# Causal attention with a gated feed-forward on one core: scores in four column groups of 32 keys, odd heads in turned order, and a new recorded order

## The chip, the cores and the metric

The kernel runs on one core of a Trainium2 chip. The metric is the device time of one execution in microseconds. Of an execution the profiler also gives a trace: which instruction ran when on which engine, and what it waited for.

## What is computed

A linear recurrence with complex decay runs over 768 steps for 4 x 8 heads of 48 channels; its result, reordered to 3072 rows of 384, goes through two weight matrices with a rational function between them.

```python
B, H, S, D = 4, 8, 768, 48                     # q, k, v, a_re, a_im: (B, H, S, D)
mag = np.sqrt(a_re * a_re + a_im * a_im)
scale = np.minimum(mag, 0.999) / (mag + 1e-06)
a_re_n, a_im_n = (a_re * scale, a_im * scale)
for t in range(S):
    S_re, S_im = (ar * S_re - ai * S_im + k_t v_t^T, ar * S_im + ai * S_re)
    y[:, :, t] = np.einsum('bhd,bhde->bhe', q[:, :, t], S_re)
x = y.transpose(0, 2, 1, 3).reshape(B * S, H * D)
h = x @ w_in                                   # (3072, 384) @ (384, 2048)
P = a[0] + a[1] * h + a[2] * h**2 + a[3] * h**3
Q = 1.0 + np.abs(b[0]) * np.abs(h) + np.abs(b[1]) * h**2
out = (P / (Q + 1e-06)) @ w_out                # (3072, 2048) @ (2048, 384)
```

## The kernel before, in words

The 768 steps are cut into six chunks of 128, and each chunk with each of the four batches is a unit, 24 in all. Two units make a pair, and each pair has one feed-forward pass over its 256 rows.

A unit goes through four helpers. `norm` (L441) loads `AA`, normalizes the decay and runs its product along the chunk. `angle` (L471) sums the angles. `outer` (L509) loads `QK` and `V`, forms the rotated queries and keys and writes them by DMA into `HQ`, whose 96 used partitions are 2 x 48 channels. `attn` (L539) is the part that the change touches. For each of two groups of four heads it transposes the keys (`turn`, L552) into `kT`, then forms the scores of 128 keys by 128 queries (`scores`, L563), which VectorE multiplies by the mask `cmask` out of PSUM into `ST`. `values` (L581) multiplies the scores by `V` and, from the second chunk on, the queries by the state `St`; these matmuls write 32 output partitions each, in four column groups of the array. L585 forms the state's update out of `kT` and `V`, again 32 output partitions at a time. `ffn` holds the two feed-forward matmuls, L613 into `ph` and L630 into `po`, with the rational function on ScalarE and VectorE between them.

Every fp32 matmul call leaves two records in the trace (384 records at L563 for 24 x 2 x 4 calls).

All steps are operations of a plan: each has a list of the engines that could run it with an assumed cost, and reads and writes that order it. The order of all 2,731 operations, and the engine of each, is not worked out at run time but stands in the string `ORDER`, which `recorded` (in the listing) decodes: base85, inflated, 16-bit steps; of a sum the lower 12 bits are the operation's number, the rest the place of its engine in the operation's list. If the string fits the plan, its order is taken and the assumed costs play no part. Each engine executes its operations in that order.

PSUM tiles of `attn` come from a ring named `at` with two buffers of one bank each.

Of the kernel before, what the change touches and what calls it, by code (L numbers as in the profile page):

```python
# [42 lines left out]
VP = 64  # L43
STAGE = ("wh0", "g", "wh1", "g", "wh2", "g")
# [171 lines left out]
def act(n, psum=False):  # L216
# [11 lines left out]
    "GRstTugEM7K99&7@|oTOgW}>-r=8N3d+9Qee8y@g`I4$c%VOyz4?>e<89QH=GCb#Nj8~x18ZN50Bw8QHU9F_QOOzJ#d<_GwU!@rM7Bj!Q`#RDr<}d4*A<mQh"
    "P-XA7F4Hku0Q!~5x4d^h6w(~gnES4ngv(3R=vCdQe@bz=8yXy+o)yO3-sWQ$Cx5W}BbqP0bdwY{x7{$EODx5S`!ntpkq5e2!nBJ#F7xG<P9yuGQbm$<orb{w"
    "arw8rsB5Gfne37F>e(~?5zxvZ>j5!&Zj}t;{cd_2#B#Xmr`x16D|gTjwVW3&&zTKw1~o~S!AiBwO~0nZ*%5w>H-uG7gMA7ZgvsZunXF0D58SWo1FdLhx=6{4"  # L230
    "Nyy2LDe&K+@)f*(y2C4>oprhws|)p{deWGE;=I?ifsA11rE)4XSDHu<@8i%Z@ED?vWta@mW%8kBnl;XWnWN$*<P}{F0|#@pMCOulr1aqJ3z8Zd?d=Mkr(%`m"
    "n%0nux>nxNi(H-7W7<oO>k4mP=%W6m6=6yzaK9{Xhi+<ZJI)oC5xUZ5xhS1!-garcwMbsq>e9h`KlBmVS7o)2WE!<llkP^sws?EVU(Y`IGAR^kN9L>z&5%AC"
    "FI%LOro!|2`k6Mdy>imD9C5Uh#yZ1h>molB?rhNR5=jir<Ol60zv)pO2v3K)yHsVlj*+EWPZr1rtk6tqpoR?CenSJD{;DTUzMn$v7wCST7$LRDYd>)v)#f<C"
    "WprL%`$!2HEc0}WCR+9P=_r`DO<$7bCdwtttMU>1JR)D|E*YmM^gFm%1%7qLWxC01Tg88<gFw{jO8vra^N(s>)?2ERWV0@mw#3#}#-Z1hnkaj0HKHj69tGOP"
    "zT&sXNxI0>`m3Gk-@}`B5>*%ZQHSyT=UQ4eNIkfBR$A#T)7^z|yL;?<mkbWtd44K+?xs#%{MT7?x{j7>p`WCcS?)^7C|RS|WsNz6BZbLaxIaRQqPq7@n)KD<"
    "ZWXMGk3X38l}YhO%0itiPvS<saE=<%m27&+Dm1nOuSnIC(p=VSEmoXskNB%JMLyP{cD<jY@9KH(_LMs8)W@GJJ>_woA=AO>m^toulb7JZWPK7J>974*H&^@M"
    "vHMJC_lv$sRaZ-_oQ-)eXPBPVzs#@xAsvEe?1kwq;c`EDhREKK-{KZ#t-yyjYX|vRKektIua*O_t(u%PwcH=t6z99h|Ih1ql(<al*u8F{c86E*Yj0^uy^fmZ"
    "ZX<8sL)qaH1u7No0=Hd1*8Vbpr+zjw5bUFps_TiMJ5lY@TK0nPv=xlHsw1?wZRRSn!$Ex-79Z3B_~>DMU|P96lj~p9rzF57PfwWB{xEt{f;?fiy7xg+b%}1W"
    "YyDU_I9|TcS+=u3h(0z6j;y3wJ<V7buV?53Wo3)jrtfSbqMhRDmvo57WH^2`TX)%Yel-bd|BG7GP?z^cqr-M)Kc2H+4~TDG(7pKCl*0Or!?{!C6xkH$JoBtO"
    "sgFr>o9>6h;mvS&vz(*@Hn6#V7V3<a>e2`#$LUo$qDM?)_dJ!)*T(ig{y45Y880WO@U^(utdjJyhI$N?he&HyPSb{R43?i#-?Y?+t}Pjt#a(xruI`>zgFzjs"  # L240
    "dpK(QPS3{Na~)99U%1iN=3SSeRpVP^ZPs?I`2@=BVr#kG+Lf56;~(wGJBn}Kk&Q9QIXmg>PfA8ix13CL-c3fc?;71_m-vzN<TqszF?2-nrFq+v3EJI0@T*7y"
    "PBo8eF9GQhaAUoB-W|eEuIorR=Id7ZR+pRJE<kL84kz{@teXG_D$yDC=}x-YM|Pi|jVE3(!^!qvtaj97YFGT{cg-;4+!9mH^}{<m+a>OVt~E7XNg{d*^x8^0"
    "Ft1B}K96ga)yKB;2XNOz2Rl(^2ReCm@SFn5&0te;YFrmZKhJdo>Y1-I^@vvV(zFG>mB>m>K`D*Nqn12H|D49tmo!%XkI5z+eJ`ME?w~R=aO(~Fr0wGJG>xg|"
# [12 lines left out]
    "+HWpx%|7=I44P${y2ECL`xpIpHyr&IG^dg`{;uos^+{CxkX~St*r`|e+XTm$Plp-AeEfuK1a|o-vA(^-<lKU}X)VrD9+k!N+*LkNTst#R4*9`Zx-3d~h?^hw"
    "+rZBKoMewMy+ld_iI0CgYZ{K(QYzaUx4(r^Z?ak=`-vaS7vp8Pndx3<-fJqGO<2xUO=J$Agu@(Sdij4mpI{<Pz<-M}t=<8j<M8k@m^}~2%Tk%j?D8c%t7<<("
    "y>vM|=qaYVN_g0M`gp1~kxtaRHyP#WulV4<wGqyA1Ai<4>uU6fqxusXm_dd;aLj$w;XJ5!M7QUt?i|@*deDJ-GHVWEmpr&|oNpo|l_|YAihG8hGLmVsI6l{w"
    "sedY{9zpXvb%WjR|I^HNfwzy+E4G+hkJCP+m)@d=$<*qA&L+DbwFi~2;L4-e5%|m?-c82!s}f@u{4D5>cksCgfj_3aOOmxHZ3JB~P))4NM=#Ck=<CTb$!7YT"
    "?0CK_h$InPF1THTE3IXb)YYc;B(v>HVAL2*3}C8gYQtO=vW-F|o%o!`GY;UP4v&qHL-G$I%Frg9^S(2!-H)t?3*c@|G{e5)g30hS@0OIMrj$!5Jk4y<km=;^"  # L260
    "=plVwvWTP{+PK0*H59~dYVgaz8anI(bb1A}I-;s@dD%Yg*9VzgeVH2WLe*uNJnAu@{EZmv75++eg5KEyel#b_EKYK(m?TbczUqOpqCmJNy62?LZqYnlz<F`3"
    "1XIborlFfhB#$wP-7r1fHo8Ls_1K|TVaz}{8HqEe^XxY`eK84GzcFCA3wqF6aA?eovCQ80fB4_8OL@$RZ}N>-IOBV0D)7X+dK;ICkYCIg_XWzhLq#6)Ml4g~"
    "_TYCdW|;<fP8+h>#%bhH_Z1!!OJAwS`LsOiTti70xED?x{~+Fc-G&!c#$|WG-HLeT2~^yXC%2MEG$__)?<o4+V{m0VtSK#*jVE>7rNW33<s2TG&fFHsvq{{!"
    "ZnpV7SvPp6NugR+-~bU|Frjb~h=i4Wag+_A1ztIj?2i(aX{?SU;pjt%JUBfS=x=24K67mWHLO8Ao0*7ex!||EC^>KLpzs2C{sO-F6Dt0RXJY7g7wCyeC@l=O"
    "W)fK(YWC!JzOBpuOA}Lt!e3P?^Y%$jAC)EE-G*@r1|`U#At(k{9`(72v&M3L1>A$*4Qg_Aw-B2G4H$3}HIzhM<!l*PdX@?W(Va&BL6%W`A5_4T@5v+|j%K67"
    "r&;NHs+e0?iGVx#rmWj$UUFY+WlqX%sAmk0l&^uJg7tEVvKH%CU?Mt;dlnE=F4$+|=7I9^K_ikA?ZZN5+)_t`hD!ehKKc0Cr3Y1tL`raa%7@X#QC*Z2hYcP)"
    "d|-;X;NuZxaojCL9g0%B2O3nslm7yi-+c@"
# [4 lines left out]
def attn_moe(ctx: ExitStack, tc: tile.TileContext, qk, aa, v, w_in, w_out, coef, heads, lanes, out):  # L272
# [10 lines left out]
    cmask = cst.tile([P, P], F32, name="cmask")  # L283
    make_identity(nc, cmask)
    nc.scalar.activation(ident, cmask, AF.Copy)
    nc.gpsimd.memset(cmask, 0.25)
    nc.gpsimd.affine_select(out=cmask, in_=cmask, pattern=[[1, P]], compare_op=ALU.is_ge,
                            fill=0.0, base=0, channel_multiplier=-1)
    smask = cst.tile([P, 2 * NJ, C], BF16, name="smask")
    nc.vector.memset(smask, 1.0)  # L290
    nc.vector.memset(smask[:, :, 0:1], 0.0)
# [10 lines left out]
    for x in HQ:  # L302
        nc.gpsimd.memset(x[96:P, :, 1, :].bitcast(U32), 0)
# [10 lines left out]
    bad = cst.tile([P, 1], mybir.dt.int32, name="bad")  # L314

# [193 lines left out]
    def outer(c, bb):  # L509
# [7 lines left out]
        u.V = V = buf(wk, [P, H * VP], F32, "V", VB)  # L517
# [4 lines left out]
        dma(lambda: V.t, lambda: v[c, bb], (), (V,), 262, tail=3300)  # L522
# [402 lines left out]
```

## Time and profile before

| | |
|---|---|
| three runs | 637.4, 640.5, 646.07 us; median 640.5 |
| profiled execution | 640.79 us, span of its trace 639.1 us |
| instructions in the trace | 14379 |
| mean granted TensorE clock | 0.976 of full speed |

The span reaches from the first to the last recorded instruction; 1.7 us of the execution lie around it. PE is TensorE's matmuls, PEld its weight loads, DVE VectorE, ACT ScalarE, POOL GpSimd, SP the engine that issues most DMAs. Helpers record most VectorE instructions under L330 and ScalarE instructions under L342 or L336, so groups are told apart by their tiles.

### The profile page before, as it was taken

How to read it: one execution, taken by the hardware profiler on the slowest of the kernel's cores; microseconds unless marked ns; L12 is line 12 of the kernel's file. 1: busy time of each engine (PE TensorE's matmuls, PEld its weight loads, DVE VectorE, ACT ScalarE, POOL GpSimd, SP SyncE). 2: the span in 40 equal slices, each digit the busy share in tenths (PEclk: the TensorE clock that was granted, in tenths of full speed). 3: DMA queues.
4: the chain of work that ended last, by engine and by line, in shares of the span. 5: the costliest groups of instructions: out<-in, count | busy, mean ns of one | idle time of the engine just before them, and what ended most of it. 6: DMA issues, size and time to landing. Idle time of an engine off the chain costs nothing. (4 is left out here: it accounts for less than half of the span.)

```text
span 639.1 us, 14379 instructions
## 1 busy us (share of the span) xinstructions
PE 561.1 (88%) x5634; PEld 520.6 (81%) x5634; DVE 570.8 (89%) x1006; ACT 513.9 (80%) x879; POOL 269.6 (42%) x225
## 2 busy tenths in 40 slices
PE   0047978799989999998999999999998999999993
PEld 0046744577779999997999999999988999999993
DVE  8898998899999999998999999999898977978683
ACT  6645899699978978986988999899787797767870
POOL 1301332416567677365446463572634553100210
PEclk9996997899999999998999999999999999999997
DMA  7689514545191243244262460552644122510000
GB/s 287 199 187 278 165 43 100 117 125 131 35 170 43 67 94 86 66 107 88 49 168 54 89 157 26 105 130 60 123 76 92 52 66 67 102 40 2 1 26 30
DMA packets 39100, 62.36 MB, mean 98 GB/s; under 512 B 4464, under 2 KB 26224, under 8 KB 39024
## 3 DMA queue, kind: packets, MB, share of 16 engines
q1 hardware_dynamic: 37872, 60.31, 38.8%
q10 hardware_dynamic: 1152, 1.05, 0.7%
q8 instruction: 46, 0.75, 0.5%
q14 instruction: 30, 0.25, 0.1%
HBM read 37.75 MB, written 4.72 MB: 66 GB/s over the span
## 5 line engine op out<-in xcount | busy, mean ns | idle before, releaser
L630 PE MATMUL po<-wh,g 128*128 128x384 f32 x640 | 179.3, 340 | 1.6 <-ACT ob L336 1.6
L613 PE MATMUL ph<-xT,wiH 128*128 128x256 f32 x960 | 162.7, 288 | 2.9 <-DVE A L330 2.9
L330 DVE SCALAR_TENSOR_TENSOR A<-A,co,z 128x512 f32<-128x512 f32 x176 | 130.9, 744 | 34.3 <-ACT z L342 32.1
L630 PE MATMUL po<-wo,g 128*128 128x384 f32 x428 | 149.5, 391 | 7.4 <-DVE g L330 7.4
L613 PEld LDWEIGHTS ph<-xT,wiH 128*128 128x128 f32 x960 | 136.6, 191 | 5.6 <-DVE A L330 2.9
L613 PE MATMUL ph<-xT,wi 128*128 128x256 f32 x632 | 125.6, 318 | 1.0 <-DVE A L330 0.6
L330 POOL TENSOR_TENSOR g<-A,g 128x512 fp32r<-128x512 f32 x47 | 64.5, 1378 | 130.7 <-DVE g L674 62.3
L630 PEld LDWEIGHTS po<-wh,g 128*128 128x128 f32 x640 | 117.1, 188 | 2.5 <-ACT ob L336 1.7
L613 PEld LDWEIGHTS ph<-xT,wi 128*128 128x128 f32 x632 | 101.9, 194 | 9.9 <-DVE A L330 2.6
L342 ACT ACTIVATE z<-A,co 128x512 f32<-128x512 f32 x96 | 66.4, 692 | 44.4 <-DVE A L330 38.1
L630 PEld LDWEIGHTS po<-wo,g 128*128 128x128 f32 x428 | 80.9, 192 | 23.0 <-DVE g L330 10.4
L330 DVE SCALAR_TENSOR_TENSOR A<-A,co,ph 128x512 f32<-128x512 f32 x96 | 71.0, 741 | 3.4 <-ACT A L342 3.4
L342 ACT ACTIVATE A<-A,co 128x512 f32<-128x512 f32 x96 | 69.5, 724 | 3.8 <-DVE g L330 1.8
L342 ACT ACTIVATE A<-ph,co 128x512 f32<-128x512 f32 x96 | 65.3, 683 | 7.7 <-DVE A L330 6.6
L330 DVE SCALAR_TENSOR_TENSOR z<-A,z 128x512 f32<-128x512 f32 x96 | 66.4, 692 | 1.9
L552 PE MATMUL at<-ident,HQ 128*128 128x128 f32 x160 | 19.9, 258 | 47.2 <-DMA HQ<-Q 41.6
L342 ACT ACTIVATE A<-ph 128x512 f32<-128x512 f32 x96 | 56.8, 592 | 5.1 <-PE ph L613 4.7
L552 PEld LDWEIGHTS at<-ident,HQ 128*128 128x128 f32 x160 | 16.7, 143 | 50.6 <-issue 44.2
L342 ACT ACTIVATE z<-z 128x512 f32<-128x512 f32 x96 | 56.3, 587 | 1.5
L563 PE MATMUL at<-HQ 96*128 96x128 f32 x384 | 53.9, 289 | 1.3 <-ACT kT L336 1.1
L563 PEld LDWEIGHTS at<-HQ 96*128 96x128 f32 x384 | 50.5, 203 | 3.2 <-ACT kT L336 2.4
L330 POOL TENSOR_TENSOR QK<-QK,RU 128x768 f32<-128x768 f32 x18 | 35.5, 1973 | 31.4 <-DMA QK<-in_qk 22.5
(173 smaller groups left out, 954.7 us busy)
## 6 DMA issues: line engine op xcount, KB each, us to landing
HQ<-Q SPq DMA_DIRECT2D x136, 128.0 KB, 4.5
AA<-in_aa SPq DMA_DIRECT2D x23, 384.0 KB, 3.2
QK<-in_qk SPq DMA_DIRECT2D x23, 384.0 KB, 5.2
V<-in_v SPq DMA_DIRECT2D x24, 256.0 KB, 4.5
wh<-in_w_in SPq DMA_DIRECT2D x6, 512.0 KB, 5.8
wh<-in_w_out SPq DMA_DIRECT2D x8, 384.0 KB, 4.0
g<-in_w_out SPq DMA_DIRECT2D x8, 384.0 KB, 5.6
g<-in_w_in SPq DMA_DIRECT2D x6, 512.0 KB, 4.5
```

What stands on the lines that cost most here:

```text
L330: call = lambda e: getattr(e, kind)(*map(real, args), **{k: real(x) for k, x in kw.items()})
L342: plan.op(dict(ACT=(act(n, psum) + more, lambda e: e.activation(o(), i(), f, **kw))), r, w)
L552: e.transpose(pt[:, i].bitcast(F32R), hq[:, 4 * g + i, 1, :], ident)
L563: e.matmul(pst[:, i, :], hf[:, 4 * g + i, 1, :], hf[:, 4 * g + i, 0, :], start=True, stop=True)
L613: e.matmul(ph[:, x * T:x * T + T].rearrange("p (h t) -> p h t", h=nb), wt[f // 4 * NJ + j][:, f % 4 * P:f % 4 * P + P], xT[:, x0:x0 + nb, ...
L630: e.matmul(po[b][:, 0:DM], gg[:, b * C:b * C + C], wt[:, 0:DM], start=(f == 0 and n == 0), stop=(f == NFF - 1 and n == len(prods) - 1))
```

## The change

Scores: a head's 128 keys are cut into four blocks of 32. Block y is one matmul with 32 output partitions, and since a key is used only by queries that are not earlier, it streams only the queries from 32y on: 128, 96, 64 and 32 columns. For even heads block y lands in column group y, for odd heads in group 3 - y. The parts of PSUM that nothing writes are masked by zero, so the two banks of the ring `at` are now two fixed tiles, zeroed once at the start by VectorE.

The keys of an odd head thus stand in turned order of their blocks, and the mask has a second half for them, now in bf16. `V` has a third part: even heads as before, odd heads in natural order without padding for the state's update, and odd heads in turned order for `values`; 704 columns instead of 512. The slow path for other inputs reads a second copy, `vn`.

Transposes use 96 partitions instead of 128, so that `HQ`'s other 32 need no zeros. `smask` becomes uint8, `ob` narrower. Four assumed costs of the plan are changed, and `ORDER` is another string.

```diff
+EV, OD = H // 2 * VP, H // 2 * D
+VW = 2 * EV + OD
...
 ORDER = (
...
-    cmask = cst.tile([P, P], F32, name="cmask")
+    cmask = cst.tile([P, 2, P], BF16, name="cmask")
...
+    for y in range(4):
+        part = cmask[32 * y:32 * y + 32, 1]
+        nc.gpsimd.affine_select(out=part, in_=part, pattern=[[1, P]], compare_op=ALU.is_ge,
+                                fill=0.0, base=32 * y - 96, channel_multiplier=-1)
...
-    for x in HQ:
-        nc.gpsimd.memset(x[96:P, :, 1, :].bitcast(U32), 0)
...
+    banks = [ps.tile([P, 512], F32, name=f"bank{i}") for i in range(2)]
+    for x in banks:
+        nc.vector.memset(x, 0.0)
...
-        u.V = V = buf(wk, [P, H * VP], F32, "V", VB)
+        u.V = V = buf(wk, [P, VW], F32, "V", VB)
...
+    def at(shape):
+        x = buf(ps, shape, F32, "at", 2)
+        bank = banks[(len(plan.rings["at"]) - 1) % 2]
+        x.make = lambda: bank[:, 0:shape[1] * shape[2]].rearrange("p (a b) -> p a b", b=shape[2])
+        return x
...
-                        e.transpose(pt[:, i].bitcast(F32R), hq[:, 4 * g + i, 1, :], ident)
...
+                        e.transpose(pt[:, i].bitcast(F32R), hq[0:96, 4 * g + i, 1, :], ident[0:96, 0:96])
...
-                    e.matmul(pst[:, i, :], hf[:, 4 * g + i, 1, :], hf[:, 4 * g + i, 0, :], start=True, stop=True)
...
+                    for y in range(4):
+                        m = 32 * (3 - y if i % 2 else y)
+                        e.matmul(pst[m:m + 32, i, 32 * y:C], hf[:, 4 * g + i, 1, 32 * y:32 * y + 32], hf[:, 4 * g + i, 0, 32 * y:C],
+                                 start=True, stop=True)
...
-                        l = V[:, m:m + 32] if q is None else St[0:96, bb].rearrange("p h d -> p (h d)")[:, m:m + 32]
+                        n = m - VP * h + VP * (h // 2) + (EV + OD + 16 if h % 2 else 0)
+                        l = V[:, n:n + 32] if q is None else St[0:96, bb].rearrange("p h d -> p (h d)")[:, m:m + 32]
...
-                    e.matmul(pd[y:y + 32, h], kT[:, h, y:y + 32], V[:, VP * h:VP * h + D], start=True, stop=True)
...
+                    n = EV + D * (h // 2) if h % 2 else VP * (h // 2)
+                    e.matmul(pd[y:y + 32, h], kT[:, h, y:y + 32], V[:, n:n + D], start=True, stop=True)
```

Decoded, both strings hold the same 2,731 operations. On TensorE the 48 score blocks and 24 blocks of values stand among feed-forward and transpose blocks. In the new order two score blocks follow each other directly 11 times, and a score block is followed directly by values twice. In the old order values are never next to each other, so the blocks in column groups make 24 runs there; in the new one, where scores belong to them too, 59.

The engines of the operations that have a choice (number before and after):

| line before | what | DVE | POOL | ACT |
|---|---|---|---|---|
| 398 | sign of a folded weight | 18, 17 | 10, 11 | |
| 411 | low part of a weight | 11, 6 | 17, 22 | |
| 458 | sum of squares | 13, 10 | 11, 14 | |
| 461 | scale factor | 3, 3 | 7, 3 | 14, 18 |
| 462 | `T` of `AA` | 10, 6 | 14, 18 | |
| 469 | carry `ncar` | 13, 5 | 11, 19 | |
| 486 | `CO` wrapped | 5, 3 | 7, 9 | |
| 490 | carry `thc` | 2, 3 | 8, 7 | |
| 525, 528 | `Z`, `RU` | 9, 8 and 7, 8 | 15, 16 and 17, 16 | |
| 529 | `QK` times `RU` | 6, 8 | 18, 16 | |
| 555 | `kT` out of PSUM | 10, 7 | | 30, 33 |
| 673 | high part of `g` | 29, 31 | | 51, 49 |
| 675 | low part of `g` | 33, 32 | 47, 48 | |
| 688 | output out of PSUM | 11, 9 | | 15, 17 |

In sum VectorE has 946 and then 922 operations, ScalarE 811 and 818, GpSimd 214 and 231.

## Rows read from the trace of the kernel before

**Rows 1.** The page's first part, each engine's busy time, share of the span and instructions, and from its second part TensorE's busy tenths in 40 slices of the span.

```profile
PE 561.1 (88%) x5634; PEld 520.6 (81%) x5634; DVE 570.8 (89%) x1006; ACT 513.9 (80%) x879; POOL 269.6 (42%) x225
...
PE   0047978799989999998999999999998999999993
```

**Rows 2.** Busy time by stages: the stage and its length, then busy time (and instructions) of PE, PEld, DVE, ACT and POOL, the granted clock, the DMA engines' busy share, GB/s.

```profile
0.00:120.00 120.00, 64.74 (x396) 47.99 (x400) 110.58 (x235) 87.87 (x149) 33.38 (x38) 0.93 0.61 177
120.00:160.00 40.00, 39.09 (x358) 30.63 (x350) 36.74 (x67) 34.85 (x62) 14.40 (x13) 0.96 0.50 122
160.00:480.00 320.00, 309.71 (x3577) 296.97 (x3566) 302.75 (x509) 280.24 (x485) 180.07 (x148) 0.99 0.41 89
480.00:600.00 120.00, 118.11 (x1140) 115.97 (x1140) 96.32 (x151) 92.25 (x153) 37.81 (x26) 1.00 0.25 56
600.00:639.00 39.00, 29.43 (x191) 29.01 (x189) 24.44 (x48) 18.65 (x32) 3.91 (x3) 0.92 0.07 23
```

**Rows 3.** The chain of waits that ended last, in order of time: start of a piece, its length from the end of the piece before to its own end, engine, tile and line, records.

```profile
501.16 0.89 PE at L563 x8
502.05 1.06 PE po L630 x6
...
508.23 1.04 PE po L630 x6
509.27 1.06 PE ph L613 x9
510.34 1.89 PE at L581 x64
512.22 1.26 PE ph L613 x9
...
577.68 1.89 PE at L581 x64
579.57 4.36 PE po L630 x24
...
615.71 13.02 PE po L630 x75
```

**Rows 4.** The timeline of TensorE in short windows: start of the first record, time from it to the end of the last one, and their number. The first two rows and the last two are from windows of some 0.1 and 0.2 us at the borders of a block of values, where a merged row holds only the records that touch the window.

```profile
510.06 0.28 PE L613 MATMUL ph<-xT,wiH 128*128 128x256 f32 x1
510.27 0.32 PE L581 MATMUL at<-ST,V 128*32 128x128 f32 x4
...
511.17 1.06 PE L581 MATMUL at<-HQ,St 96*32 96x128 f32 x32
...
468.29 0.86 PE L585 MATMUL at<-V,kT 128*32 128x48 f32 x48
...
511.93 0.29 PE L581 MATMUL at<-HQ,St 96*32 96x128 f32 x4
512.15 0.50 PE L613 MATMUL ph<-xT,wiH 128*128 128x256 f32 x2
```

**Rows 5.** The records of one line: shortest, median and longest duration in ns, first and last start, shape; and the group of the transposes with their weight loads (records | busy us, mean ns of one | idle before, releasers).

```profile
L581 PE MATMUL at<-HQ,St x640: 270/272/276, 159.9 to 579.3; 96*32 96x128 f32 x160
L585 PE MATMUL at<-V,kT x960: 203/206/288, 47.4 to 488.5; 128*32 128x48 f32 x192
...
L552 PE MATMUL at<-ident,HQ 128*128 128x128 f32 x160 | 19.9, 258 | 47.2 <-DMA HQ<-Q 41.6 <-DVE St L330 3.4 <-DVE A L330 1.3
L552 PEld LDWEIGHTS at<-ident,HQ 128*128 128x128 f32 x160 | 16.7, 143 | 50.6 <-issue 44.2 <-DVE St L330 3.9 <-DVE A L330 1.6
```

**Rows 6.** Busy time of L563 alone by stages (PE and PEld with records, clock, DMA share, GB/s), first stage and sum.

```profile
0.00:120.00 120.00, 9.99 (x48) 8.92 (x48) 0.93 0.61 177
...
sum 639.00, PE 53.89 PEld 50.48; mean PE 10.78 PEld 10.10
```

**Rows 7.** Groups of instructions on VectorE and, last, one on GpSimd: line, engine, operation, tiles, shapes and count | busy us, mean ns of one | idle before, releasers.

```profile
L330 DVE TENSOR_TENSOR ST<-at,cmask 128x512 f32<-128x512 f32 x48 | 32.2, 682 | 6.0 <-PE at L563 5.8
L330 DVE TENSOR_TENSOR SQ<-SQ 128x384 f32<-128x384 f32 x12 | 7.3, 610 | 0.8 <-ACT SQ L342 0.8
L330 DVE TENSOR_TENSOR T<-AA,SQ 128x384 f32<-128x384 f32 x9 | 5.8, 648 | 1.3 <-ACT SQ L342 1.3
L330 DVE COPY ncar<-MM 128x3 f32<-128x3 f32 x13 | 4.0, 307 | 0.0
L330 DVE TENSOR_TENSOR wi<-wi,wiH 128x512 fp32r<-128x512 f32 x6 | 4.4, 736 | 0.0
L330 DVE TENSOR_TENSOR wo<-wo,wh 128x384 fp32r<-128x384 f32 x3 | 1.6, 543 | 0.0
L330 DVE TENSOR_SCALAR kT<-at 128x384 f32<-128x384 f32 x10 | 5.5, 550 | 0.8 <-PE at L552 0.8
L330 DVE TENSOR_SCALAR CO<-CO 128x768 f32<-128x768 f32 x5 | 2.8, 553 | 0.0
L330 DVE TENSOR_TENSOR QK<-QK,RU 128x768 f32<-128x768 f32 x5 | 4.7, 946 | 0.0
L674 DVE CAST g<-A 128x512 fp32r<-128x512 f32 x29 | 12.9, 446 | 0.3
L330 DVE TENSOR_TENSOR g<-A,g 128x512 fp32r<-128x512 f32 x33 | 26.8, 815 | 0.2
L330 DVE TENSOR_SCALAR wo<-po,co 128x384 f32<-128x384 f32 x4 | 2.5, 613 | 0.0
L300 DVE MEMSET St<- 96x2048 f32 x1 | 1.8, 1765 | 0.4 <-issue 0.4
...
L330 POOL TENSOR_TENSOR T<-AA,SQ 128x384 f32<-128x384 f32 x14 | 14.9, 1067 | 18.7 <-ACT SQ L342 12.7 <-ACT RU L342 5.9
```

**Rows 8.** The page's sixth part, DMA issues (KB each, median us from issue to landing), and the DMA line of its second part.

```profile
V<-in_v SPq DMA_DIRECT2D x24, 256.0 KB, 4.5
...
DMA packets 39100, 62.36 MB, mean 98 GB/s; under 512 B 4464, under 2 KB 26224, under 8 KB 39024
```

More of the change, by code (lines that the diff above doesn't have):

```diff
@@ L228 @@
[L228 to L231, printed above, removed]
@@ L268, with attn_moe @@
+    "Ys)vg;I<1?)`3fW{ism#J69d{sfFJv#}r(IRsHjoKXDe9=`dN3lX+wIyH2Mf<Zqs<3Vv%_1(~(vx~XQX!d4YZX6Rw!xW{R<5l{YMVr{PaC(SH!iNFio1WnPL"
+    "FS20MB2&gjmS|cLo+ecMPUnLP|6G0&ydL5e0W-HQS+^dZtWXcp-z}y+JNx<nW9r(%62A1ctcqMV&)ch<&aTsyJ7k{2djVbd)%LdLmDIifeT-(0ps8&ADGV=J"
+    "J)EltAi@7V!^cd43AJU(pcE(4a<-HdD=$;Z`Y%WP-$@^$_Yd?Vc&3>DCvvC%`Tqf~I;ZC"
 )
 @with_exitstack
-def attn_moe(ctx: ExitStack, tc: tile.TileContext, qk, aa, v, w_in, w_out, coef, heads, lanes, out):
+def attn_moe(ctx: ExitStack, tc: tile.TileContext, qk, aa, v, vn, w_in, w_out, coef, heads, lanes, out):
@@ L282, in attn_moe @@
     ident = cst.tile([P, P], F32R, name="ident")
[L283 to L285 removed]
+    cmask = cst.tile([P, 2, P], BF16, name="cmask")
+    make_identity(nc, cmask[:, 0])
+    nc.scalar.activation(ident, cmask[:, 0], AF.Copy)
     nc.gpsimd.memset(cmask, 0.25)
[L287 removed]
+    nc.gpsimd.affine_select(out=cmask[:, 0], in_=cmask[:, 0], pattern=[[1, P]], compare_op=ALU.is_ge,
                             fill=0.0, base=0, channel_multiplier=-1)
[L289 to L291 removed]
+    for y in range(4):
+        part = cmask[32 * y:32 * y + 32, 1]
+        nc.gpsimd.affine_select(out=part, in_=part, pattern=[[1, P]], compare_op=ALU.is_ge,
+                                fill=0.0, base=32 * y - 96, channel_multiplier=-1)
+    smask = cst.tile([P, 2 * NJ, C], mybir.dt.uint8, name="smask")
+    nc.vector.memset(smask, 1)
+    nc.vector.memset(smask[:, :, 0:1], 0)
     ab = cst.tile([P, 6], F32, name="ab")
@@ L584, in values @@
                 for y in range(0, 2 * D, 32):
-                    e.matmul(pd[y:y + 32, h], kT[:, h, y:y + 32], V[:, VP * h:VP * h + D], start=True, stop=True)
-        pe((1980 if c else 1010) + (0 if last else 800), values, (V, *sts, *u.hq, ("St", bb), *(() if last else (kT,))),
+                    n = EV + D * (h // 2) if h % 2 else VP * (h // 2)
+                    e.matmul(pd[y:y + 32, h], kT[:, h, y:y + 32], V[:, n:n + D], start=True, stop=True)
+        pe((1980 if c else 1010) + (0 if last else 600), values, (V, *sts, *u.hq, ("St", bb), *(() if last else (kT,))),
            (py,) if last else (py, pd))
@@ L686, in ffn @@
                 cols = slice(h * n, h * n + n)
-                ob = buf(ff, [P, 512], F32, *(("A2", A2B) if end or whole and b else ("wo15" if b else "ob", 1)))
+                ob = buf(ff, [P, 512 if end or whole and b else DM], F32, *(("A2", A2B) if end or whole and b else ("wo15" if b else "ob", 1)))
                 evac(n, lambda ob=ob, n=n: ob[:, 0:n], lambda b=b, cols=cols: po[b][:, cols], (po[b], "co"), ((ob, h),),
@@ L870, in attn_moe @@
                                         *(("ncar", b) for b in range(B))), (("cnt", 0), ok), port=True)
-    pc = buf(ps, [P, 512], F32, "at", 2)
-    pe(60, lambda e: e.matmul(pc[0:1, 0:3], ones, cnt, start=True, stop=True), (("cnt", 0), ("cnt", 1)), (pc,))
+    pc = at([P, 4, C])
+    pe(60, lambda e: e.matmul(pc[0:1, 0, 0:3], ones, cnt, start=True, stop=True), (("cnt", 0), ("cnt", 1)), (pc,))
     plan.op(dict(DVE=(300, count)), (pc,), ("bad",))
@@ L900, in values, with turned @@
         return np.pad(x, [(0, 0)] * 4 + [(0, VP - D)]).reshape(NC, B, C, H * VP)
+    def turned(x):
+        x = x.reshape(NC, B, C, H, VP)
+        odd = x[..., 1::2, 0:D]
+        back = np.pad(odd.reshape(NC, B, 4, C // 4, H // 2, D)[:, :, ::-1].reshape(odd.shape), [(0, 0)] * 4 + [(VP - D, 0)])
+        return np.concatenate([y.reshape(NC, B, C, -1) for y in (x[..., 0::2, :], odd, back)], axis=-1)
     rows = np.arange(DM).reshape(H, D)
@@ L907 @@
         "aa": np.stack([dense(inputs["a_re"]), dense(inputs["a_im"])], axis=3),
-        "v": values(inputs["v"]),
+        "v": turned(values(inputs["v"])),
+        "vn": values(inputs["v"]),
         "w_in": inputs["moe_w_in"].view(np.int64)[rows],
```

100 lines of the change are left out of this document (50 added, 50 removed).

## The prediction

> **What bounds the kernel now.** I read the page's first part, then busy time by stages, then the chain of waits that ended last, and last the timeline of TensorE around single blocks. Over the span VectorE (DVE) is busy 89% and TensorE (PE) 88% [rows 1]; such a share is an average over stages, so the stages matter. In the first 120 us PE is busy 64.7 of 120 and DVE 110.6: weights are unfolded, DVE is the fuller engine. From 160 to 480 us both are nearly full, PE 309.7 and DVE 302.8 of 320. From 480 to 600 PE has 118.1 of 120 and DVE 96.3, and after that only the last feed-forward pair is left [rows 2]. In its last 130 us the chain is almost only PE, block behind block with no gap, the scores of L563 among them [rows 3]. So PE time taken out behind 120 us should come back almost whole, unless DVE, some 2% less full, becomes the bound; before that a shorter PE block gives little.
>
> **Scores, term by term.** Before, a score block of four heads is 8 records and takes 0.89 us of the chain, and the feed-forward block behind it costs what it costs elsewhere (1.06 against 1.04 for six): no price for the change of shape [rows 3]. After, it is 32 records of 32 output columns. The nearest rows are L581 and L585, which already work in four (three) column groups. In L581 four records start within 0.02 us of each other, so the groups run side by side [rows 4]. A wave of four with 128 moving columns takes (1.06 - 0.27) / 7 = 0.113 us, a wave of three with 48 columns (0.86 - 0.21) / 15 = 0.043; 0.27 and 0.21 are the last record's own duration [rows 4, 5]. The straight line through both is 0.87 ns a column and 2 ns a record. The turned order of odd heads gives every group 128 + 32 or 96 + 64 = 160 columns per pair of heads; twice that for two records a call, times two pairs, is 640 columns in 16 records: 0.56 + 0.03 = about 0.58 us. Bounds: 0.53 if records cost nothing of their own and columns 0.83 ns; 0.63 if a 32-column record can't be cheaper than a 48-column one (4 such records x 0.013). I take 0.58. The 48 blocks save 48 x (0.89 - 0.58) = 14.9 us, between 12.5 and 17.3.
>
> **The price of going in and out.** L581 shows what the chain of pieces hides for L563. Going in: the last full-width record starts at 510.06, the first narrow one at 510.27, 0.21 us instead of the 0.12 (1.06 / 9) between full-width records: 0.09 lost. Going out: the nine records behind cost 1.26 instead of 1.06, and 24 of L630 4.36 instead of 4 x 1.04: 0.20 lost [rows 3, 4]. Together 0.29 us for each run of narrow blocks, as much as a score block saves. What counts is therefore how many runs the new order makes. Decoded, it has 72 narrow blocks (48 scores, 24 values) in 59 runs, since 11 times two score blocks stand together and twice one stands before values; before there were 24 runs. 35 more x 0.29 = +10.2 us. I find no cover for it: it is PE's own time. The new order saves it only where blocks touch.
>
> **Transposes.** 40 blocks of four lose 32 of 128 moving columns. If time went with columns, 160 x 0.083 x 1/4 = 3.3 us ((19.9 / 40 - 0.25) / 3 = 0.083 a transpose); if the weight load sets it, nothing. The load keeps its 128 columns and lasts 143 ns, longer than that spacing [rows 5], so I take 0.5.
>
> PE together: -14.9 + 10.2 - 0.5 = -5.2 us, between -10 and -2. Of the 48 score blocks 42 lie behind 120 us (384 - 48 of 384 records) [rows 6], so -4.6 us comes off the bound stage.
>
> **DVE and the new engines.** The decoded order takes 24 instructions from DVE. By their mean durations [rows 7]: line 411 -5 x 0.64 (mean of two shapes), 462 -4 x 0.65, 469 -8 x 0.31, 458 -3 x 0.61, 555 -3 x 0.55, 486 -2 x 0.55, 688 -2 x 0.61, 675 -0.8, 398 -0.4, against 529 +2 x 0.95, 673 +2 x 0.45 and 490 +0.2: -12.3 us (525 and 528 cancel). The two new memsets of the banks stand ahead of everything on DVE: a 96x2048 one takes 1.77, so 2 x 0.44 = +0.9, and the first HQ needs what DVE does behind them. Net -11.4. In the stage where both engines are full this only keeps DVE from taking over as the bound. In the first 120 us DVE is 92% busy; they are a quarter of the 480 us in which norms and attention run, so about 12.3 / 4 = 3 us of the relief falls there, less the 0.9. How much of the 2.1 comes back no row shows, between nothing and all; I take -1.9, since DVE is the fuller engine there. POOL takes over most of it at twice the time (1.07 against 0.65) and is at 42%, which hides it; with its cover gone it would be a late input of norm.
>
> **The rest.** V grows from 256 to 352 KB, 24 x 96 KB = 2.3 MB more on 62.4 MB. Its median landing is 4.5 us and it is issued well before values; at the 177 GB/s of the first 120 us the first two units' 0.19 MB are 1 us of queue [rows 2, 8]. Hidden, otherwise +1. The mask product keeps its 512 elements from PSUM, 0.68 us [rows 7], whatever the type of the mask. The fixed banks keep the two-deep ring, so I count no new wait.
>
> Sum: 640.8 (this execution) - 4.6 - 1.9 = 634.3, say 634. The median of the runs shown is 640.5, the same within 0.05%, so the prediction stands against it too.
>
> **Rivals.**
> *The switches are paid for elsewhere or are cheaper, and both engines' relief comes through.* Then it is the full 14.9 x 42/48 = 13.0, with 1 of the transposes' 3.3 and 3 in the first stage: 640.8 - 13 - 1 - 3 = about 624. For it: in the stage from 160 to 480 DVE is relieved as well, and the rows show the switch at L581 alone. Against it: the 0.20 behind L581 is the same in front of L613 and of L630.
> *Nothing comes back.* DVE, at 302.8 of 320 where PE has 309.7, sets the pace with its waits, or the new order hands the 5 us back in other waits: 640.
> *Slower: unequal blocks don't overlap.* If a head's short blocks can't finish ahead of its long one, each head costs two waves of 128 columns: 8 x 0.11 = 0.88 us, no saving, and the 35 switches stay: 640.8 + 10.2 x 42/48 - 2 = about 648. It decides as soon as a block exceeds 0.68 us (0.89 - 10.2 / 48), where the PE sum turns positive. L581's waves are of equal length and can't tell. For past 2% slower, POOL's 17 further instructions would have to make norm late as well.
> The Trainium skill, "TensorE: Matmul & The Clock Gate", under "The mechanism", says that matmuls start and end strictly in program order; here that would make this rival's case. By that rule a block takes 0.88 us and the time is 648; by the line through the rows 0.58 and 634. No row of this trace has unequal blocks, so it doesn't bear the rule out or refute it.
>
> **How the numbers follow.** Forecast 634 (its own range 629 to 638, from -10 to -2 on PE): 0.50. Switches cheap, 624: 0.23. Nothing comes back, 640: 0.15. Slower, 648: 0.12. The range leaves out the lower part of the second case and most of the fourth: 623 to 643. Two per cent is about what a measurement of this kernel can tell from no change, since three runs lie between 637.4 and 646.1: faster than 628 takes most of the second case and a little of the first, 0.24; slower than 653 a third of the last, 0.05; the rest 0.71.
>
> **What would show it.** Right: score blocks alone between feed-forward blocks take about 0.67 us in the chain (0.09 + 0.58) with 0.20 more on the block behind, two together about 1.25; PE's busy time falls by a few us, DVE's to about 559, POOL's rises; the chain's last part is still PE. Wrong: score blocks of 0.88 (unequal blocks wait for each other), feed-forward blocks behind them at 1.06 (no switch price, so the time goes to 624), or a chain that runs through DVE or HQ's DMAs behind 480 us (the order lost what the blocks won).

## The result and the profile after

| | median | runs | ratio to before, 95% interval |
|---|---|---|---|
| before | 640.61 us | 637.4 to 646.07 | |
| after | 619.92 us | 618.21 to 621.97 | 0.967, 0.9595 to 0.9744 |
| forecast | 634.0 us | 623 to 643 | |

The change takes 20.7 us off, 3.3%, and the time after lies below the forecast range. The profiled execution of after has a span of 620.2 us. First the page's lines on the engines and on TensorE's busy tenths, against [rows 1].

```profile
PE 552.5 (89%) x6786; PEld 506.8 (82%) x6786; DVE 561.2 (90%) x984; ACT 515.7 (83%) x886; POOL 278.9 (45%) x244
...
PE   0048868899999999999999999899999999999994
```

PE is busy 8.6 us less than before, VectorE 9.6 us less, GpSimd 9.3 us more. The stages, with the columns of [rows 2], show where the time is won:

```profile
0.00:120.00 120.00, 66.72 (x678) 50.29 (x679) 112.42 (x238) 91.56 (x159) 33.08 (x48) 0.96 0.66 187
120.00:160.00 40.00, 38.79 (x425) 29.99 (x424) 39.29 (x67) 37.59 (x65) 25.79 (x21) 1.00 0.53 114
160.00:480.00 320.00, 315.85 (x4365) 298.92 (x4364) 297.13 (x501) 287.67 (x497) 199.44 (x162) 0.99 0.42 97
480.00:600.00 120.00, 120.00 (x1258) 116.83 (x1258) 102.97 (x158) 94.78 (x161) 19.34 (x15) 1.00 0.22 50
600.00:639.00 39.00, 11.18 (x66) 10.75 (x64) 9.35 (x23) 4.15 (x8) 1.30 (x1) 0.89 0.07 22
```

From 160 to 480 us PE now works 315.9 of 320 us where it had 309.7, and ScalarE 287.7 where it had 280.2 [rows 2]. In the middle of the kernel TensorE is kept busier, while VectorE is busy for 5.6 us less there.

The chain of waits that ended last, as in [rows 3] (start, length, what):

```profile
482.83 0.68 PE bank L579 x17
483.51 1.28 PE ph L632 x9
484.80 1.05 PE po L649 x6
...
489.93 1.07 PE ph L632 x9
...
495.20 1.89 PE bank L599 x64
497.09 1.24 PE po L649 x6
...
552.64 1.24 PE bank L579 x34
553.88 2.36 PE ph L632 x18
```

This is what the forecast said of the blocks: a lone score block (L579, before L563) takes 0.68 us and the nine records behind it 1.28 instead of 1.07; two that touch take 1.24. A lone block thus costs 0.68 + 0.21 = 0.89 us, exactly what a block cost before [rows 3]. Only touching blocks save.

Ahead of 480 us the chain of before tells something that [rows 3] does not show. Four of its pieces:

```profile
455.40 0.70 ACT z L342
456.12 0.59 ACT z L342
456.74 0.76 DVE A L330
457.52 0.70 DVE z L330
```

Of the 80 us from 400 to 480, the pieces on TensorE make up only 6 us before; 70 us are ScalarE and VectorE, which hand tiles to each other. (Further back than 398 us this chain can't be followed.) So there TensorE was nearly full by its busy share, and yet it was not what the end waited for.

The waits of one engine for another tell the rest. Each line: who, for whom, us in total, times, longest. Before, on ScalarE, VectorE and TensorE:

```profile
ACT z L342 <- DVE A L330: 38.1, 38, 3.1
...
DVE A L330 <- ACT z L342: 32.1, 37, 2.7
...
PE po L630 <- DVE g L330: 7.4, 3, 4.2
PE at L581 <- DVE ST L330: 6.8, 4, 3.4
```

After, the same four:

```profile
ACT z L350 <- DVE A L338: 18.5, 25, 2.3
...
DVE A L338 <- ACT z L350: 17.7, 22, 3.2
...
PE bank L599 <- DVE ST L338: 3.5, 3, 1.4
...
PE po L649 <- DVE g L338: 2.0, 1, 2.0
```

The rational function passes its tiles back and forth between ScalarE (z) and VectorE (A). These hand-overs cost 70 us of idle time before and 36 after, and TensorE's two waits for their product and for the scores fall from 14 to 5.5 us. Not every wait falls: VectorE's wait for the other tile that ScalarE hands it, A, grows from 3.4 to 9.4 us. Nothing in the new scores touches the rational function. That points to the order string, which the forecast had valued at 1.9 us.

### The profile page after: what moved, and what is told of

The parts are those of the page before. It is cut to its first block, busy times and chain, and to the rows that moved or that the text cites. A ratio compares the mean times of both kernels' runs of the same rounds, so it can differ in the third digit from the quotient of the medians.

```text
span 620.2 us, 16732 instructions
## 1 busy us (share of the span) xinstructions
PE 552.5 (89%) x6786; PEld 506.8 (82%) x6786; DVE 561.2 (90%) x984; ACT 515.7 (83%) x886; POOL 278.9 (45%) x244
## 4 chain that ended last, share of the span: by engine, by line
PE 64%; DVE 20%; DMA 7%; ACT 4%; issue 3%; SPq 1%; POOL 0%; ACTq 0%; DVEq 0%; POOLq 0%
PE po L649 26%; PE ph L632 26%; PE bank L599 5%; PE bank L579 4%; DVE A L338 4%; DMA HQ<-Q 3%; DVE T L338 3%; DVE MM L338 2%; PE bank L566 2%; PE bank L604 1%; DVE wo L338 1%; DVE z L338 1%; DVE wi L338 1%; ACT A L350 1%; DMA AA<-in_aa 1%
## 5 line engine op out<-in xcount | busy, mean ns | idle before, releaser
L649 PE MATMUL po<-wh,g 128*128 128x384 f32 x640 | 181.4, 340 | 0.0
L338 DVE SCALAR_TENSOR_TENSOR A<-A,co,z 128x512 f32<-128x512 f32 x176 | 130.5, 742 | 20.1 <-ACT z L350 17.7
L632 PE MATMUL ph<-xT,wi 128*128 128x256 f32 x632 | 128.3, 322 | 7.2 <-DVE A L338 4.1
L350 ACT ACTIVATE z<-A,co 128x512 f32<-128x512 f32 x96 | 66.3, 690 | 21.8 <-DVE A L338 18.5
L566 PE MATMUL bank<-ident,HQ 96*128 96x96 f32 x160 | 19.5, 260 | 44.1 <-DVE wh L338 36.2
L566 PEld LDWEIGHTS bank<-ident,HQ 96*128 96x128 f32 x160 | 17.1, 147 | 47.1 <-issue 42.3
L579 PEld LDWEIGHTS bank<-HQ 96*32 96x32 f32 x1536 | 32.8, 117 | 10.3 <-issue 3.0
L338 DVE TENSOR_TENSOR ST<-bank,cmask 128x512 f32<-128x512 f32 x48 | 32.0, 683 | 8.8 <-PE bank L579 8.3
L579 PE MATMUL bank<-HQ 96*32 96x32 f32 (+3 forms) x1536 | 37.8, 248 | 1.4 <-ACT kT L344 1.1
```

The source lines that it names most:

```text
L338: call = lambda e: getattr(e, kind)(*map(real, args), **{k: real(x) for k, x in kw.items()})
L350: plan.op(dict(ACT=(act(n, psum) + more, lambda e: e.activation(o(), i(), f, **kw))), r, w)
L566: e.transpose(pt[:, i].bitcast(F32R), hq[0:96, 4 * g + i, 1, :], ident[0:96, 0:96])
L579: e.matmul(pst[m:m + 32, i, 32 * y:C], hf[:, 4 * g + i, 1, 32 * y:32 * y + 32], hf[:, 4 * g + i, 0, 32 * y:C], start=True, stop=True)
L632: e.matmul(ph[:, x * T:x * T + T].rearrange("p (h t) -> p h t", h=nb), wt[f // 4 * NJ + j][:, f % 4 * P:f % 4 * P + P], xT[:, x0:x0 + nb, ...
L649: e.matmul(po[b][:, 0:DM], gg[:, b * C:b * C + C], wt[:, 0:DM], start=(f == 0 and n == 0), stop=(f == NFF - 1 and n == len(prods) - 1))
```

## The experiments

Two theories stood at the start. *Order:* the new order list removes waits between the engines, whatever the scores. *Scores:* the narrow blocks save more than forecast, through PE or what they release. Kernels below are named by what they take from before and after; where only the order list differs, the diff is given in words, since the list is a packed string.

### Which part carries the gain

```diff
 narrow_old_order: after's computation
-ORDER = the list of after
+ORDER = the list of before
 wide_new_order: before's computation
-ORDER = the list of before
+ORDER = the list of after
```

> All of the change except the recorded order: scores in column groups, under the order and engines of before. Theory 'order': a score block alone between feed-forward blocks costs as much as a wide one (0.90 against 0.90 us with its switches, read off the two traces), and only touching blocks save 0.32 us each; the old order has 9 touching pairs of score blocks and 4 in front of values, so 13 x 0.32 = 4.2 us and a little for the transposes: 635 to 638 us. Theory 'scores': the shorter blocks free their readers earlier and bring most of the 20 us by themselves: 625 or less.

> Only the new recorded order, on the kernel before with its wide scores. Theory 'order': it brings about 15 of the 20 us: 623 to 628 us, with the idle gaps of TensorE from 160 to 330 us gone as in the changed kernel. Theory 'scores': 636 to 642, since the order was made for shorter blocks.

narrow_old_order: 640.34 us, ratio to before 1.0041 (1.0 to 1.0083), above both forecasts. wide_new_order: 625.27 us, 0.9819 (0.9745 to 0.9893). Before, measured beside them, took 639.33. The order alone brings 14.1 us (by the interval 7 to 16), the scores alone nothing, and the scores on top of the new order 625.27 - 619.92 = 5.4 us, where the 619.92 was measured at another time. The two parts therefore don't simply add up: the order is worth 14 us with the wide scores and 640.34 - 619.92 = 20 us with the narrow ones. The waits of wide_new_order are close to those of after although its scores are the wide ones of before:

```profile
ACT z L339 <- DVE A L327: 19.6, 26, 2.3
...
DVE A L327 <- ACT z L339: 15.4, 22, 2.1
...
PE po L627 <- DVE g L327: 4.3, 1, 4.3
...
PE at L578 <- DVE ST L327: 2.7, 3, 1.7
```

and those of narrow_old_order are those of before:

```profile
ACT z L347 <- DVE A L335: 38.2, 39, 3.1
...
DVE A L335 <- ACT z L347: 34.3, 36, 3.6
```

The engines' busy time in wide_new_order and then in narrow_old_order:

```profile
PE 556.7 (89%) x5634; PEld 520.6 (84%) x5634; DVE 564.4 (91%) x982; ACT 514.5 (83%) x885; POOL 280.1 (45%) x242
```

```profile
PE 555.2 (88%) x6786; PEld 506.0 (80%) x6786; DVE 567.8 (90%) x1008; ACT 514.6 (81%) x880; POOL 262.5 (41%) x227
```

The span of wide_new_order, 623.4 us, is 15.7 shorter than that of before. TensorE's idle time falls by 11.3 of these (639.1 - 561.1 = 78.0 against 623.4 - 556.7 = 66.7), and its busy time by 4.4 with the same 5634 matmuls; why those 4.4 fall is open. In narrow_old_order the narrow scores do take 5.9 us off TensorE's busy time, but the median time stays. The number of runs can't be the reason, since with narrow scores the old order also makes 59 (72 blocks, of which 9 touch a score block and 4 stand before values). The chain offers one: from 400 to 480 us TensorE's pieces make up 10 of 80 us in narrow_old_order, against 78 in wide_new_order, and 26 and 45 in the two profiles of after (after and after_again). By this reading TensorE was not what was waited for in this stretch under the old order, so shorter blocks there had little to give back.

So the theory of the scores fell, and with it the question moved to what in the order list does it: the engines that it names, the sequence, the lighter VectorE, or its early or late part.

```diff
 narrow_new_seq_old_eng
-order: (operation, engine) as in after
+order: operations as in after; 229 operations on before's engine
 narrow_old_seq_new_eng
+order: operations as in before; 229 operations on after's engine
```

> The changed kernel with the new sequence of operations, but each of the 229 operations whose engine differs back on its engine of before. If the moves from VectorE to GpSimd and ScalarE carry the gain of the order: 632 to 638. If the sequence carries it: 621 to 626. If the two only fit together, it is slower than the changed kernel by more than either alone would explain, 640 or more.

> The changed kernel with the sequence of before and the engines of the new order. If the engine moves carry the gain: 621 to 626. If the sequence does: 634 to 640. If the two only fit together: 640 or more.

653.85 us, ratio 1.0284 (1.0199 to 1.0369), and 677.01 us, 1.0621 (1.054 to 1.0703). Neither half brings anything by itself, both lose: a sequence with the other list's engines doesn't fit. These two runs can't say which of the two carries the gain, for further down a list with 63 small moves already costs 17 to 22 us.

```diff
 dve_load
+    scr = cst.tile([P, 1], F32, name="scr")
...
-        for o in plan.order(ROUNDS):
+        for n, o in enumerate(plan.order(ROUNDS)):
             o.emit(E)
+            if 150 <= n < 2550 and n % 96 == 0:
+                nc.vector.tensor_reduce(scr, flat(smask)[:, 0:384], AX.X, ALU.max)
```

> The changed kernel with 25 further instructions on VectorE, one after every 96th operation from the 150th to the 2550th of the order, each reading 384 mask bytes into one element that nobody reads: about 0.4 to 0.5 us each, 10 to 12 us in all, as much as the new engines took off it. If the gain of the order is VectorE's lighter load, it gives that back: 628 to 632. If the gain is that hand-overs between ScalarE and VectorE are covered better, the further work fills idle time: 620 to 624.

622.37 us, 0.9729 (0.9679 to 0.9779): 25 more VectorE instructions of 541 ns, 13.5 us, cost 2.4 us against the 619.92 of after. As much load as the new order takes from VectorE, put back at 25 evenly spread places, takes back little of the gain.

```diff
 new_then_old
+order: the first 1494 operations as in after, the rest as in before
 old_then_new
+order: the first part as in before, the rest as in after
```

> The changed kernel with the new order and engines for the first 1494 operations (to about 340 us, where all but two of the first 1494 operations are the same set in both orders) and the order of before for the rest. The traces put all of the gain ahead of 340 us; if that is right: 620 to 624. If the later part carries its share (TensorE idles 3.9 us less behind 340): 626 to 632.

> The other way round: order of before for the first 1494 operations, the new one for the rest. If the gain is made ahead of 340 us: 634 to 640. If the later part carries its share: 628 to 633.

627.67 us, 0.983 (0.9776 to 0.9885), and 634.18 us, 0.9932 (0.9896 to 0.9968). Against before (640.12 beside them) some 12 us lie in the early part and 6 in the late one; neither part holds the gain alone.

### The scores: unequal blocks and fewer runs

```diff
 unturned: odd heads in the same group order as even ones
...
-                        m = 32 * (3 - y if i % 2 else y)
+                        m = 32 * y
...
```

The mask and the turned part of `V` follow the same order.

> The changed kernel with odd heads in the same group order as even ones, so that column group 0 takes 4 x 128 columns in two records each and group 3 4 x 32. If the groups run on by themselves, a score block lasts as long as its fullest group, 8 x 0.11 = 0.88 us instead of 0.60, so 0.28 more for each of the 42 blocks behind 120 us: 11 to 12 us if TensorE is the bound there, 630 to 633. If unequal blocks of one head wait for each other in the changed kernel anyway, turning saves nothing: 619 to 622.

632.02 us, 0.9884 (0.983 to 0.9937): 12.1 us more than after. One piece of the chain of unturned, two touching score blocks, and then its row among TensorE's groups (behind the bar busy us and mean ns):

```profile
562.13 1.86 PE bank L579 x34
```

```profile
L579 PE MATMUL bank<-HQ 96*32 96x128 f32 (+3 forms) x1536 | 53.6, 252 | 1.0 <-ACT kT L344 1.0
```

where after has 1.24 for two touching blocks, and in its groups

```profile
L579 PE MATMUL bank<-HQ 96*32 96x32 f32 (+3 forms) x1536 | 37.8, 248 | 1.4 <-ACT kT L344 1.1
```

Without the turn, group 0 always gets 128 columns and group 3 always 32, and a block takes as long as its fullest group. With it the groups share out evenly. Were blocks to wait for each other across groups, the turn could not matter; so a group whose short block has ended goes on while a long one still runs.

```diff
 joined, joined_again: ten pairs, as at one place of after's list
-TensorE: scores (4 heads) ... 15 operations ... scores (4 heads)
+TensorE: scores (4 heads), scores (4 heads)
```

> The kernel after with its order list changed so that ten more pairs of score blocks touch (49 runs of narrow blocks in place of 59). If TensorE sets the pace and the price lies in going in and out of narrow blocks (two lone blocks 2 x 0.90 us, two that touch 1.47), 10 x 0.32 = 3.2 us come off: 616 to 618. If the places of the score blocks are what keeps other work fed (the order's hand-overs are the gain), moving them costs as much or more than it saves: 620 to 626.

> The kernel joined once more (49 runs of narrow blocks in place of 59), in five rounds beside after_again. If each touching saves 0.32 us of TensorE on the path: 616 to 618, 2 to 4 below after_again. If the places of the blocks matter as much: within 1 of it.

> The kernel after as it is, to stand beside joined_again: 618 to 622.

joined 619.12 us (0.9634, 0.9542 to 0.9726) against after's 619.92, measured at another time; measured side by side, joined_again 617.72 (613.49 to 619.56) and after_again 618.5 (614.61 to 620.88). The 0.8 us have the forecast sign, but are a quarter of the 3.2 and can't be told from nothing. TensorE's busy time does fall, by somewhat more than the 3.2: 549.6 us in after_again, 545.2 in joined_again, by one profile of each. What takes it back is not shown. No measurement shows joined to be better than after.

### Hand-overs or any move at all

The first theory of the order was narrow: between ScalarE's square of z and VectorE's next step on A, the list of after has no other VectorE instruction in 33 of 96 chains, that of before in 48. The theory is that such an instruction fills VectorE's wait for ScalarE. Three kernels moved this number.

```diff
 new_emptied (after's list; 63 such moves, 96 chains with none between)
 ScalarE  scal(AF.Square, 512, tz, tz, ...)
+VectorE  stt(512, t2, t2, q0, tz, ...)
 VectorE  ... one to five others ...
-VectorE  stt(512, t2, t2, q0, tz, ...)
 old_filled, new_filled (40 and 31 moves the other way)
 ScalarE  scal(AF.Square, 512, tz, tz, ...)
+VectorE  one other, from behind
 VectorE  stt(512, t2, t2, q0, tz, ...)
-VectorE  one other
```

> The kernel after with its order list changed in 63 of the 96 activation chains: VectorE's step on A is put directly behind ScalarE's square, so that no VectorE instruction stands between the two in the list, in any chain (33 before the edit, 96 with it). Theory that the new order gains by putting other VectorE work into the hand-over from ScalarE: VectorE's idle time ahead of those steps grows from 18 us to 40 us or more, and the time to 628 to 635. Rival, that the gain lies elsewhere and the engines catch up: 619 to 622.

> The kernel before, wide scores and its own order, but in 40 of its 96 activation chains one VectorE instruction from further on stands between ScalarE's square and VectorE's next step (chains with none between: 48 before the edit, 8 with it). Hand-over theory: VectorE's idle time ahead of these steps falls from 32 us to 20 us or less and a part of the order's 14 us comes: 630 to 636. Rival, that hand-overs have slack and the gain lies elsewhere: 638 to 646.

> The kernel after with 31 more activation chains given one VectorE instruction between ScalarE's square and VectorE's next step (chains with none between: 33 before the edit, 2 with it). Hand-over theory: VectorE's idle time ahead of these steps falls below 18 us and the time to 615 to 619. Rival, hand-overs have slack: 619 to 623.

new_emptied: 641.73 us, 1.0031 (0.9999 to 1.0063), 22 us more than after. old_filled: 644.98, 1.0063 (1.0019 to 1.0106). new_filled: 627.37, 0.9775 (0.9695 to 0.9855), 7 us more than after. The first agrees with the hand-over theory in sign and goes beyond its range (VectorE's wait for z rises from 17.7 to 35.9 us, a little less than forecast); the other two contradict it. The waits of new_filled point to why filling didn't pay:

```profile
DVE A L335 <- ACT A L347: 14.3, 19, 1.6
DVE A L335 <- ACT z L347: 9.5, 13, 3.2
...
ACT z L347 <- DVE A L335: 31.9, 32, 2.6
```

VectorE's wait for z falls from 17.7 to 9.5 as meant, but ScalarE's wait for VectorE rises from 18.5 to 31.9: one reading is that the filler only delays the step that ScalarE needs next. And new_emptied could be no hand-over effect at all, if any move in the list costs as much. A control moved as many VectorE instructions over the same distances, none of them a hand-over.

```diff
 new_nudged (after's list; 63 moves of VectorE instructions of norm, outer, fold, angle, attn)
+VectorE  line 481 of norm
 VectorE  line 416 of fold
 VectorE  line 416 of fold
-VectorE  line 481 of norm
 old_emptied (before's list; as new_emptied, 48 moves)
```

> The kernel after with 63 VectorE instructions that belong to no activation chain moved ahead in the order list past as many VectorE instructions (one to five) as in new_emptied, so that the number of VectorE instructions between ScalarE's square and VectorE's next step stays what it was in every chain. If new_emptied's 22 us came from the hand-overs: 620 to 627. If any such move in a fitted order costs as much: 635 to 645.

> The kernel before, wide scores and its own order, with VectorE's step directly behind ScalarE's square in the other 48 chains too (96 of 96). If fillers in the hand-overs are worth what new_emptied lost (22 us for 63 chains, 0.35 each): 640 + 48 x 0.35 = 657, 650 to 662. If the old order has no hand-overs to lose because other waits set its pace: 638 to 646.

new_nudged: 635.71 us, 0.9973 (0.9939 to 1.0007), 17 us more than after_again. old_emptied: 660.64, 1.0388 (1.0319 to 1.0458), 22 us more than before. In the new list moves that leave every hand-over's filler alone cost most of what new_emptied cost, so there the narrow theory is not needed for the larger part. old_emptied falls where the hand-over theory put it (650 to 662), and VectorE's wait for z rises in it from 32.1 to 49.9 us; but moves without a hand-over were not tried in the old list, so it can't tell the two apart.

The trace of new_nudged shows another cause. Its page:

```profile
PE 555.9 (88%) x6786; PEld 508.1 (80%) x6786; DVE 573.3 (90%) x984; ACT 516.8 (81%) x886; POOL 280.2 (44%) x244
```

VectorE is busy 12 us longer than in after with the very same 984 instructions (in new_emptied, at 573.6 us, as well). One group holds 5.5 us of it (mean ns of one in the second place): in after

```profile
L338 DVE TENSOR_SCALAR MM<-SQ 128x384 f32<-128x384 f32 x23 | 10.7, 464 | 0.1
```

and in new_nudged

```profile
L335 DVE TENSOR_SCALAR MM<-SQ 128x384 f32<-128x384 f32 x23 | 16.2, 704 | 1.3 <-POOL SQ L335 1.1
```

The shortest, median and longest of that group in new_nudged:

```profile
L335 DVE TENSOR_SCALAR MM<-SQ x23: 347/353/1984, 7.4 to 474.2; 128x384 f32<-128x384 f32 x23
```

and the timeline around the longest one (start, us, engine, what):

```profile
121.94 1.94 POOL L335 TENSOR_TENSOR QK<-QK,RU 128x768 f32<-128x768 f32 x1
...
122.12 1.98 DVE L335 TENSOR_SCALAR MM<-SQ 128x384 f32<-128x384 f32 x1
...
124.14 0.84 ACT L347 ACTIVATE SQ<-SQ 128x768 f32<-128x768 f32 x1 [1.23 <-DVE MM L335]
```

An instruction that takes 353 ns at the median lasts 1.98 us beside a GpSimd instruction, ends 0.22 us after it, and ScalarE waits 1.23 us for it. To test whether this is what moved instructions pay, GpSimd's work was shortened in both orders:

```diff
 after_fill, nudged_fill
-    E = dict(ACT=nc.scalar, DVE=nc.vector, POOL=nc.gpsimd, PE=nc.tensor, SP=nc.sync)
+    class Fill:
...
+        def tensor_tensor(self, out, *args, **kw):
+            nc.gpsimd.memset(out.bitcast(F32), 1.0)
+    E = dict(ACT=nc.scalar, DVE=nc.vector, POOL=Fill(), PE=nc.tensor, SP=nc.sync)
...
-        e.tensor_scalar(bad[0:1], nok[0:1], P * (4.0 * NC * B + B * NJ + 10.0) - 0.5, None, ALU.is_le)
+        e.tensor_scalar(bad[0:1], nok[0:1], -1e30, None, ALU.is_le)
```

These kernels leave out GpSimd's two-input arithmetic, and the last line keeps them from branching to the slow path for other inputs.

> The kernel after, but every two-input GpSimd instruction of the fast path only fills its output tile with a constant, so GpSimd's work is a fraction of its 279 us; order and all other instructions as they are, the outputs are not the reference's. If VectorE is held up beside GpSimd instructions, its busy time falls from 561 us to about 540 (22 us lie in 30 lengthened instructions), and the time to 605 to 618. If not, VectorE stays at 558 to 563 and the time at 612 to 620.

> The kernel new_nudged with the same edit (GpSimd only fills; outputs are not the reference's). If collisions with GpSimd are what the 63 moves cost (17 us, VectorE 12 us busier), VectorE's busy time comes down to that of after_fill within 2 us and the time to within 6 of after_fill. If the moves cost by waits between VectorE, ScalarE and TensorE, it stays 12 to 17 us above after_fill.

after_fill: 616.3 us (0.9646, 0.9576 to 0.9717). nudged_fill: 618.98 us (0.9693, 0.9622 to 0.9763). The 17 us between the two orders shrink to 2.7. Their pages, after_fill and then nudged_fill:

```profile
PE 545.8 (89%) x6786; PEld 501.9 (82%) x6786; DVE 544.9 (89%) x984; ACT 515.0 (84%) x886; POOL 121.1 (20%) x244
```

```profile
PE 550.0 (89%) x6786; PEld 504.7 (82%) x6786; DVE 545.7 (89%) x984; ACT 515.8 (84%) x886; POOL 121.5 (20%) x244
```

VectorE's 12 us of difference are 0.8. So the 63 moves of new_nudged cost through GpSimd; for the other moved lists this was not tried. What the edit can't part is an instruction held up beside GpSimd from one that waits for a late result of GpSimd, since a fill shortens both; that from after to new_nudged VectorE's busy time grows by 12 us and its waits for POOL only from 0.4 to 2.1 speaks for the first. In the order of after the 16 us of VectorE time bring only 2 to 4 us: from 160 to 480 us TensorE is busy 319.6 of 320 us in after_fill, so it is the bound there.

## Why the prediction was wrong, point by point

**What bounds the kernel now** was right for the stage behind 480 us, where TensorE has 118.1 of 120 us before and 120.0 after. For 160 to 480 us it took PE's 309.7 of 320 as full and concluded from the chain's last 130 us that PE time taken out behind 120 us comes back almost whole. From 400 to 480 us the chain of before ran through ScalarE and VectorE, with 6 of 80 us on TensorE (and once more for some 9 us at 526), and under the old order nothing of the scores' saving came back (narrow_old_order).

**Scores, term by term** and **The price of going in and out** were right to 0.01 or 0.02 us: 0.68 in the chain (forecast 0.67), 1.24 for two (1.25), 0.21 more on the block behind (0.20). That what counts is the number of runs was right for TensorE's busy time (4.4 us less for ten runs fewer, forecast 3.2 in the experiment); of the kernel's time ten runs fewer took 0.8 us, which can't be told from nothing.

**Transposes**: their group falls from 19.9 us [rows 5] to

```profile
L566 PE MATMUL bank<-ident,HQ 96*128 96x96 f32 x160 | 19.5, 260 | 44.1 <-DVE wh L338 36.2 <-DMA HQ<-Q 4.6 <-DVE g L338 2.4
```

that is 0.4, forecast 0.5. For all of PE the forecast was 5.2 us less busy time; between kernels that differ in the scores alone it is 5.9 under the old order (561.1 to 555.2) and 4.2 under the new one (556.7 to 552.5). PE's share of the forecast time, -4.6, measured -5.4 under the new order. Under the old order it measured 0.

**DVE and the new engines**: -11.4 forecast, 570.8 to 561.2 is -9.6. That so little of it comes back agrees with dve_load: 13.5 us put back cost 2.4. GpSimd's 1.07 against 0.65 us is 1.6 times as long, not twice.

**The step that failed** is the worth of the new order. The order list was valued by the instructions that it moves off VectorE alone (-1.9). The prediction's part "The rest" reads "The fixed banks keep the two-deep ring, so I count no new wait", and no term of the sum stands for waits that go. By wide_new_order, with the wide scores of before and no other edit, the order is worth -14.1 us; the scores then bring the 5.4. In the trace of wide_new_order it shows as waits that go: the hand-overs between ScalarE and VectorE cost 35 us where they cost 70 before, and TensorE's two waits 7 where they cost 14. All of these waits stood in the trace of before and could have been read as what a better order may win. The rival "Nothing comes back" had waits in it with one sign only, as something that a new order may add.

**The rivals.** "Switches cheap, 624" came nearest by its number, and that is luck: the switches cost what was forecast. "Slower" fell: unequal blocks do overlap, as unturned shows from the other side. The rule of the Trainium skill, "TensorE: Matmul & The Clock Gate", "The mechanism", that matmuls start and end strictly in program order, does not decide the length of a block here: by it a block would take 0.88 us, and it takes 0.68 with the way in, so the measurement decides.

**What stays open.** Which property of the new list removes the waits. VectorE's lighter load by itself does not explain it (dve_load), it doesn't sit in one part of the list alone (the two halves), and more fillers in the hand-overs don't bring it (old_filled, new_filled). Whether the engines or the sequence carry it was not parted. It isn't a smaller loss beside GpSimd on balance either, as far as VectorE's busy time shows: its fall of 9.6 us is less than the 11.4 us of instructions that left it. Whether wide_new_order and before, both with GpSimd's work shortened, would still differ was not tried.

## What to carry to other kernels

Waits in the trace are a reserve that a new order can draw on: before valuing an order by the instructions that it moves, add up the idle time of each engine behind the others in the stage that counts, and give the order a range between nothing and that sum. Read the chain of waits in the middle of the kernel too, and not only its end: an engine that is 97% busy there need not be the one that is waited for. Test an order and a computation apart, each under the other's partner, since a saving on TensorE is worth nothing where another wait ends last (here 5.9 us of busy time brought nothing). In a recorded order like this one a move of one to five places cost a quarter of a microsecond on average (17 us for 63), so an edit that "only" shifts VectorE instructions wants a measurement of its own.

## What the runs showed of the hardware

A VectorE instruction of 353 ns lasted up to 1.98 us beside a GpSimd instruction, and the same 984 instructions took 561.2 us in one order, 573.3 in another, and 545 in both once GpSimd's instructions were short. The Trainium skill, "SBUF — State Buffer", "SBUF: two separate sides", says that the two engines share a pair of ports as an exclusive lock: where VectorE's instruction runs in a two-port mode, or has two inputs in SBUF against a GpSimd instruction that reads SBUF, the one that starts first holds the pair for its whole instruction and the other blocks. The timeline above agrees with that: VectorE's instruction began 0.18 us after the GpSimd one and ended 0.22 us after it. In which mode it ran, no trace here shows.

Narrow blocks of four unequal lengths run on in their column groups by themselves: a score block's time goes with what its fullest group carries (0.62 us with 160 columns per pair of heads in after, 1.24 / 2; 0.93 with 256 in unturned, 1.86 / 2).
